# The opening of a gated-attention and FFN kernel: state sums of units 0 to 3 as prefix sums in PSUM, and another split and order of the first weight conversions

## The chip, the cores and the metric

The kernel runs on one core of a Trainium2 chip. The metric is the device time of one execution in microseconds (us). A core has a matrix engine (TensorE, PE in the rows, its weight loads PEld), a vector engine (VectorE, DVE), an activation engine (ScalarE, ACT), GpSimd (POOL) and SyncE (SP), which issues most transfers. TensorE writes to PSUM, eight banks of 2 KB for each of 128 partitions; the other engines read it from there.

## The reference

A recurrence over 768 positions for 4 batches of 8 heads of 48 dimensions, and then a feed-forward layer with a Gelu on the 3072 rows of 384 that come out:

```python
for t in range(S):
    state = alpha[:, :, t, :, None] * state + einsum('bhd,bhe->bhde', k[:, :, t], v[:, :, t])
    y[:, :, t] = einsum('bhd,bhde->bhe', q[:, :, t], state)
x = y.transpose(0, 2, 1, 3).reshape(B * S, H * D)
h = x @ w_in                                  # 384 -> 2048
out = (0.5 * h * (1 + erf(h / sqrt(2)))) @ w_out
```

## The kernel before

**Units.** The 3072 rows are 12 groups g of 256 positions, three to a batch; a group is two units (u = 0, 1) of four heads, so there are 24 units n. For a unit, VectorE makes running products of alpha forward (two scans of 256, L320) and backward (L333), multiplies q by the forward one (L326) and k by the backward one (L339). TensorE makes the scores in four chunks of 64 positions and turns k round (L360, L368). VectorE masks the scores (L427), ACT copies the turned k (L421). `inside` then multiplies the scores by v (L450) and, in the same bank, makes for each chunk j the sum of k times v over the chunk, 48 columns for each of 16 small matmuls (L469). These run on four quarters of the array, two halves of the rows by two halves of the columns. `chain` on VectorE adds the four sums up one after the other into the states before chunk 1, 2, 3 and after chunk 3 (L487 for the first of a batch, L489). `outer` multiplies q by these states (L519) and adds them to the bank. `carry` (L494) takes the last state to the next group.

**x.** What `inside` and `outer` leave in a unit's bank is x. It is used as two roundings, a high half (ACT copy, L599) and a low half, the rest: by VectorE as a difference (L603), or "by product": TensorE subtracts the high half from the bank with a matrix of -1 (L612) and ACT copies what is left (L616). `X_BY_PRODUCT` lists the units that do the second. A small transfer spreads spare rows of x (L625) before a step of the group can start.

**Weights.** w_in and w_out come as 16 pieces a to p of 768 KB, in turns (a is w_in's first, b w_out's first). Each is converted by ACT (top bits, L274), VectorE (join, L278), ACT (high half, L288), and its low half by VectorE (L291) or, for the pieces in `BY_PRODUCT` (numbers 1, 2, 3: b, c, d), by TensorE, four records of an identity matmul and two of a subtraction (`differ`, L300 and L301), and two ACT copies (L305). The two top buffers are used in turns, so the conversion of a piece starts behind the join of the piece two before it.

**Steps.** A step (g, f) multiplies a group's x by the pair of pieces f (L635, 18 matmuls of 256 columns), takes a Gelu, and multiplies by w_out's pieces (L844). Step (0, f) needs pieces 2f and 2f+1, f = 1 thus c and d. The high half of x of unit 2 waits for the low halves of pieces a to e, since its place is theirs before.

**Order.** A planner in the kernel fixes each engine's order ahead of time. Each operation has a cost (`COST`), what it depends on, and a rank; at each moment of the plan an engine takes the ready operation with the lowest rank (a negative rank is urgent work, for which VectorE and ACT may be kept idle for a moment). Ranks come from the place in the string `ORDER`: digits are units, letters pieces. SP's loads and fetches use the same ranks. Engines then work through their lists in that order, with waits where data come late. While no step has begun, TensorE is kept busy with matmuls of no use (`turn_over`, L140).

Of the kernel before, what the change touches and what calls it, by code (L numbers as in the profile page):

```python
# [8 lines left out]
F32 = mybir.dt.float32  # L9
# [7 lines left out]
ALU = mybir.AluOpType  # L17
# [2 lines left out]
STAGE = 3  # L20
SHIFT = 3
WARM = (1, 1, 4, 4, 2, 2)
BY_PRODUCT = (1, 2, 3)
EARLY = 2
JOINED = 5
FLIPPED = 6
SEAM = 0.22
HOLD = 0.35
U_RANK, HI_RANK = 0.5, 0.4
X_BY_PRODUCT = (1, 2)  # L30
STEPS_BY_PRODUCT = 2
LOOK, EARLY_LOOK = 1.5, 1.0
RATE = 360.0
XB = 3
# [1 line left out]
SLOW = 1.0  # L36
COST = dict(
    turn=0.3, head=0.75, body=0.95, tail=0.49, sel=0.6, sel2=1.0, ends=0.22, differ=1.2, half=0.34, minus=0.4, gminus=0.35, rest=0.5, rest2=1.0,
    scan=0.65, scan2=0.65, back0=0.86, back=0.71, times=0.62, q=1.35, scores=1.24, scores1=0.69, flip=0.72, over=0.56, move=0.35, moves=1.4, kn=0.52, mask=0.62, mask1=0.4, kn1=0.36, inside=1.28, chain=1.1, outer=0.77, carry=0.22,
    xh=0.6, xl=0.72, spread=2.0, check=0.85, load=2.6, fetch=0.4, u=1.0, c0=0.56, c1=0.89, c2=0.56, c3=0.95, c4=0.92,  # L40
    hi=0.82, lo=0.89, gemm1=2.12, gelu=0.51, low=0.62, most=1.4, last=0.69, part=1.0,
    wide1=2.1, wide2=2.07, wpart=1.1, quick1=2.45, quick2=1.42, comb1=0.36, comb3=1.08, chi=0.98, clo=1.2, wsum=0.72, wcomb=0.52, whi=0.52, wlo=0.65, gather=1.5, wend0=1.39, wend1=1.16, wend2=3.69,
)
ORDER = "0 1 a b c 2 d 3 e f 4 g h i j k 5 l m n o p"


@with_exitstack
def gla_then_gelu_ffn(ctx: ExitStack, tc: tile.TileContext, q, k, v, alpha, qg, kg, ag, vg, w_in, w_out, out):
    nc = tc.nc
    B, H, D, S = q.shape  # L50
    NF, P, NK, _ = w_in.shape
    DM, DFF = NK * P, NF * P
    NT = B * S
    C = 128
    G = 2 * C
    CS = C // 2
    NCH = G // CS
    DP = 64
    NPAIR = H // 2
    NU = NPAIR // 2  # L60
# [4 lines left out]
    GPB = S // G  # L65
# [6 lines left out]
    const = ctx.enter_context(tc.tile_pool(name="const", bufs=1))  # L72
# [40 lines left out]
    ybank = ps_y.tile([P, 2, BANK], F32, name="ybank")  # L113
# [40 lines left out]
    ends = const.tile([P, NG * NU, 2], F32, name="ends")  # L154
# [11 lines left out]

    states = []
    for u in range(NU):
        states.append([const.tile([P, 2, D], F32, name=f"state{u}_{i}") for i in range(NCH + 1)])

    mask = const.tile([P, CS], F32, name="mask")
    nc.gpsimd.memset(mask, 1.0)
    for half in range(2):
        r = slice(half * CS, (half + 1) * CS)
        nc.gpsimd.affine_select(
            out=mask[r],
# [166 lines left out]
    def ends_batch(g, j):  # L343
        return g % GPB == GPB - 1 and j == NCH - 1
# [89 lines left out]
    def inside(g, u):  # L434
        d = cur[g, u]
        ybank = y_of(NU * g + u)
        vn = vbuf[g % NB]
        spare = () if g else (0, 1)[: u + 1]
        for i in spare:
            nc.tensor.matmul(  # L440
                ybank[:, i, :G], lhsT=zeros, rhs=products[:, :G], start=True, stop=False, skip_group_check=True
            )
        for j in range(NCH):
            for i in range(2):
                r = slice(i * CS, (i + 1) * CS)
                for h in range(2):
                    rows = D if i in spare else DP
                    o = slice((h ^ i) * DP, (h ^ i) * DP + rows)
                    e = (2 * u + h) * D
                    nc.tensor.matmul(  # L450
                        ybank[o, i, j * CS : (j + 1) * CS],
                        lhsT=vn[r, j, e : e + rows],
                        rhs=d["ss"][r, h, j, :],
                        start=(j == 0 and i not in spare),
                        stop=(j == 0 and g % GPB == 0),
                        skip_group_check=True,
                    )
        if NU * g + u < FLIPPED:
            kn = d["kn"].rearrange("p b (c h d) -> p b c h d", c=2, h=2)
        for j in range(NCH):  # L460
            if ends_batch(g, j):
                continue
            t = 2 * C + j * D
            for i in range(2):
                r = slice(i * CS, (i + 1) * CS)
                for h in range(2):
                    o = slice(h * DP, (h + 1) * DP)
                    e = (2 * u + h) * D
                    nc.tensor.matmul(  # L469
                        ybank[o, i, t : t + D],  # L470
                        lhsT=d["kn"][r, h, j].rearrange("p b d -> p (b d)") if NU * g + u >= FLIPPED else kn[r, j // 2, j % 2, h],
                        rhs=vn[r, j, e : e + D],
                        start=False,
                        stop=True,
                        skip_group_check=True,
                    )

    def chain(g, u):
        d = cur[g, u]
        ybank = y_of(NU * g + u)  # L480
        st = states[u]
        for j in range(NCH):
            if ends_batch(g, j):
                continue
            new = ybank[:, :, 2 * C + j * D : 2 * C + (j + 1) * D]
            if g % GPB == 0 and j == 0:
                d["chain"] = nc.vector.tensor_copy(st[1], new)  # L487
            else:
                d["chain"] = nc.vector.tensor_tensor(out=st[j + 1], in0=new, in1=st[j], op=ALU.add)  # L489

    def carry(g, u):
        if ends_batch(g, NCH - 1):
            return
        nc.vector.scalar_tensor_tensor(  # L494
            out=states[u][0],
            in0=states[u][NCH],
            scalar=1.0 / MID,
            in1=cur[g, u]["pe"].unsqueeze(2).to_broadcast([P, 2, D]),
            op0=ALU.mult,
            op1=ALU.mult,  # L500
        )
# [7 lines left out]
    def outside_part(g, u):  # L509
        d = cur[g, u]  # L510
        ybank = y_of(NU * g + u)
        for j in range(NCH):
            if g % GPB == 0 and j == 0:
                continue
            t = slice(j * CS, (j + 1) * CS)
            for i in range(2):
                for h in range(2):
                    r, o = (slice(a * DP, a * DP + D) for a in (h, h ^ i))
                    ins = nc.tensor.matmul(  # L519
                        ybank[o, i, t],  # L520
                        lhsT=states[u][j][r, i],
                        rhs=d["qt"][r, i, t],
                        start=False,
                        stop=True,
                        skip_group_check=True,
                    )
                    tc.add_manual_dep(
                        ins.ins,
                        d["chain"].ins.name,
                        mybir.DependencyInfo(mybir.DependencyClass.Sync, mybir.DependencyReason.DATA),  # L530
                        reason="row tiles of one bank",
                    )
# [167 lines left out]
    sums = {}  # L700
# [303 lines left out]
    def op(*args, **kw):  # L1004
        ops.append(Op(*args, **kw))
        return ops[-1]

    load, ready_x, unit, wops, x_last = {}, {}, {}, {}, {}
    gemms = {}

    def plan_unit(n):
        g, u = divmod(n, NU)
        d = unit[n] = {}
        p, pp_ = unit.get(n - 1, {}), unit.get(n - 2, {})
        r = unit_rank[n]
        fns = {}
# [5 lines left out]
        old = unit.get(n - NB * NU, {})  # L1022
# [5 lines left out]
        if u == NU - 1:  # L1028
            d["load"].cost += 0.4
            d["load"].kb += 393  # L1030
        half = op("DVE", "scan", start, [d["load"], p.get("q"), p.get("keys"), p.get("ends")], rank=r)
        d["scan"] = op("DVE", "scan2", lambda: fns["f"](1), [half], rank=r)
        d["ends"] = op("ACT", "ends", lambda: fns["e"](), [d["scan"]], rank=-0.5)
        d["q"] = op("DVE", "times", lambda: fns["q"](), [d["scan"]], rank=r)
        before = unit.get(n - 3, {})
        half = op("DVE", "back0", lambda: fns["b"](0), [d["scan"], *([before["xh"], before["xl"]] if "out" in before else [])], rank=r)
        d["back"] = op("DVE", "back", lambda: fns["b"](1), [half], rank=r)
# [2 lines left out]
        of_y = [yp.get("out", yp.get(x)) for x in ("xh", "xl")]  # L1040
        if n >= FLIPPED:
            flip = op("DVE", "flip", lambda: flipped(g, u), [d["keys"], p.get("away")], rank=r)
            d["away"] = op("SP", "move", lambda: flip_out(g, u), [flip], rank=r - 50, lands=2.6, kb=262)
            back = op("SP", "moves", lambda: flip_back(g, u), [d["away"], p["kn"]], rank=r - 50, lands=4.5, kb=524)
# [31 lines left out]
        else:  # L1076
            d["mask"] = op("DVE", "mask", lambda: masked(g, u), [d["scores"], rp.get("inside")], rank=-1)
            d["kn"] = op("ACT", "kn", lambda: turned_out(g, u), [d["scores"], rp.get("inside"), d["mask"]], rank=-1)
        d["inside"] = op("PE", "inside", lambda: inside(g, u), [d["mask"], *of_y], rank=r)
        if n >= NU:  # L1080
            d["inside"].deps.append(d["kn"])
        else:
            d["inside"].soon = [d["kn"]]
        if n >= SPLIT:
            d["scores"].bank = (d["mask"],)
        d["chain"] = op("DVE", "chain", lambda: chain(g, u), [d["inside"], pp_.get("carry")], rank=-1 if n else 1.5)
        if n == 1:
            op("PE", "sel2", lambda: [selected(sbank[:, i, :G], i) for i in range(2)], [d["inside"], unit[0]["zh"]], rank=-1)
        d["outer"] = op("PE", "outer", lambda: outside_part(g, u), [d["chain"], ops[-1] if n == 1 else None], rank=r)
# [9 lines left out]
        elif g > NSB and (g - NSB) % 2:  # L1099
            k = (g - NSB) // 2  # L1100
# [67 lines left out]
    low_of, state = {}, {"g": None, "run": 0, "evac": None, "more": 0}  # L1168
# [320 lines left out]
    t = 0.0  # L1489
    idle = 0  # L1490
    while True:
        moved = False
        for e in ("DVE", "ACT", "PE", "SP", "POOL"):
            if free_at[e] <= t + 1e-9:
                o = choose(e, t)
# [13 lines left out]
        t = min(later_on)  # L1509
# [8 lines left out]
    for o in plan:  # L1518
# [5 lines left out]
        out=outside[:, n_units:],  # L1524
        in0=ends.rearrange("p n i -> p (n i)"),
# [89 lines left out]
```

## Time and profile before

| | |
|---|---|
| median of 3 runs | 486.96 us (486.9 to 487.24) |
| profiled execution | 488.16 us, its span 486.6 us |
| TensorE busy | 475.8 us, 98% of the span |
| VectorE, ACT busy | 332.3 us (68%), 223.5 us (46%) |
| granted TensorE clock, mean | 0.998 |

The span runs from the first to the last instruction. A busy TensorE is one with a matmul in flight, so it may still be filled better. The kernel has one long stretch in which TensorE is busy without a break, and an opening of some 50 us in which transfers, conversions and the first units share the engines; the change lies in the opening.

### The profile page before, as it was taken

The numbers are of one execution on the slowest core, as the hardware profiler recorded it, in microseconds if no ns is written. First come the engines' busy times: TensorE is split into PE (matmuls) and PEld (weight loads), VectorE is DVE, ScalarE is ACT, GpSimd is POOL, SyncE is SP. The second block draws the span as 40 slices with busy tenths as digits, with TensorE's granted clock in tenths as the row PEclk, the third lists the DMA queues.
The fourth block names the chain that finished last, engine by engine and source line by source line (L and its number), as shares of the span: only waits on it lengthen the run. The fifth ranks groups of instructions, "written<-read, shape, count | busy, mean of one in ns | idle before, by whom it ended". The sixth has DMA issues, their size and how long they took to land.

```text
span 486.6 us, 12615 instructions
## 1 busy us (share of the span) xinstructions
PE 475.8 (98%) x5315; PEld 414.5 (85%) x5315; DVE 332.3 (68%) x655; ACT 223.5 (46%) x426; POOL 7.4 (2%) x21
## 2 busy tenths in 40 slices
PE   8999999999999999999999999999999999999995
PEld 5778999999999999977778877888888888888883
DVE  6988999988878897888952265795555444544441
ACT  4788865354534444444442345353344343334331
POOL 2000000000000000000000000000000000000000
PEclk9999999999999999999999999999999999999999
DMA  8996674555546454564430030000010000100002
GB/s 291 394 359 220 204 245 123 164 177 179 168 145 199 151 178 123 164 208 150 128 96 1 1 126 10 9 1 1 1 66 0 1 0 1 65 1 1 1 1 72
DMA packets 33809, 53.80 MB, mean 111 GB/s; under 512 B 4272, under 2 KB 15344, under 8 KB 33744
## 3 DMA queue, kind: packets, MB, share of 16 engines
q1 hardware_dynamic: 32096, 47.86, 30.2%
q0 software_dynamic: 880, 3.93, 2.2%
q10 hardware_dynamic: 768, 1.11, 0.7%
q8 instruction: 44, 0.72, 0.6%
q14 instruction: 21, 0.17, 0.1%
HBM read 41.29 MB, written 9.44 MB: 104 GB/s over the span
## 4 chain that ended last, share of the span: by engine, by line
PE 85%; DMA 6%; ACT 4%; DVE 2%; issue 1%; ACTq 0%; SPq 0%
PE hw L652 28%; PE accw L667 12%; PE acc L844 11%; PE hp L635 10%; PE accw L760 10%; PE sbank L760 6%; DMA st<-in_moe_w_out_dram 5%; PE sbank L519 2%; PE sbank L450 2%; DMA qd<-in_qg_dram 1%; PE sbank L469 1%; ACT top L274 1%; PE sh L360 1%; DVE wil L291 1%; ACT ghi L819 1%
## 5 line engine op out<-in xcount | busy, mean ns | idle before, releaser
L652 PE MATMUL hw<-x,wih 128*128 128x512 f32 x288 | 91.1, 397 | 0.0
L819 ACT ACTIVATE ghi<-hw 128x512 fp32r<-128x512 f32 x64 | 38.1, 595 | 105.7 <-PE hw L652 105.6
L834 DVE TENSOR_TENSOR glo<-h,ghi 128x512 fp32r<-128x512 f32 x38 | 26.2, 689 | 51.8 <-ACT h L824 51.8
L652 PEld LDWEIGHTS hw<-x,wih 128*128 128x128 f32 x288 | 52.0, 188 | 10.7
L652 PE MATMUL hw<-x,wil 128*128 128x512 f32 x144 | 56.9, 395 | 0.0
L844 PE MATMUL acc<-woh,ghi 128*128 128x384 f32 x128 | 44.2, 346 | 0.9 <-ACT ghi L819 0.8
L844 PE MATMUL acc<-wol,ghi 128*128 128x384 f32 x128 | 43.1, 337 | 0.0
L834 DVE TENSOR_TENSOR glo<-hw,ghi 128x512 fp32r<-128x512 f32 x26 | 17.9, 687 | 32.6 <-ACT hw L824 32.4
L819 ACT ACTIVATE ghi<-hp 128x512 fp32r<-128x512 f32 x32 | 19.1, 596 | 43.7 <-PE hp L635 43.7
L753 ACT CAST qd<-ad 128x1024 fp32r<-128x1024 f32 x19 | 20.0, 1051 | 34.0 <-DVE ad L750 34.0
L635 PE MATMUL hp<-x,wih 128*128 128x256 f32 x192 | 35.3, 283 | 0.0
L333 DVE TENSOR_TENSOR_SCAN rp<-ad,rp,bottom 128x255 f32<-128x255 f32 x48 | 33.9, 738 | 0.9
L635 PE MATMUL hp<-two_x,wih 128*128 128x256 f32 x192 | 34.4, 280 | 0.0
L756 DVE TENSOR_TENSOR ad<-ad,qd 128x1024 fp32r<-128x1024 f32 x19 | 23.3, 1225 | 15.5 <-ACT qd L753 15.5
L320 DVE TENSOR_TENSOR_SCAN pp<-ad,bottom 128x256 f32<-128x256 f32 x48 | 30.8, 666 | 4.5 <-DMA ad<-in_ag_dram 4.5
L652 PEld LDWEIGHTS hw<-x,wil 128*128 128x128 f32 x144 | 27.0, 187 | 6.6
L667 PE MATMUL accw<-ghi,woh 128*128 128x512 f32 x78 | 31.4, 402 | 0.0
L667 PE MATMUL accw<-ghi,wol 128*128 128x512 f32 x78 | 30.6, 393 | 0.0
L635 PEld LDWEIGHTS hp<-x,wih 128*128 128x128 f32 x192 | 30.0, 189 | 0.4 <-issue 0.2
L652 PE MATMUL hw<-two_x,wih 128*128 128x512 f32 x96 | 30.0, 394 | 0.0
L635 PEld LDWEIGHTS hp<-two_x,wih 128*128 128x128 f32 x192 | 29.8, 188 | 0.0
L844 PE MATMUL acc<-woh,glo 128*128 128x384 f32 x128 | 28.7, 345 | 0.0
(251 smaller groups left out, 1087.6 us busy)
## 6 DMA issues: line engine op xcount, KB each, us to landing
st<-in_moe_w_in_dram SPq DMA_DIRECT2D x8, 768.0 KB, 7.4
st<-in_moe_w_out_dram SPq DMA_DIRECT2D x8, 768.0 KB, 7.6
qd<-in_qg_dram SPq DMA_DIRECT2D x23, 256.0 KB, 3.9
ad<-in_ag_dram SPq DMA_DIRECT2D x23, 256.0 KB, 3.2
kd<-in_kg_dram SPq DMA_DIRECT2D x23, 256.0 KB, 4.3
vn<-in_vg_dram SPq DMA_DIRECT2D x12, 416.0 KB, 6.0
fd<-fl SPq DMA_DIRECT2D x18, 256.0 KB, 2.1
kx<-fd SPq DMA_DIRECT2D x72, 64.0 KB, 3.7
```

The lines of the kernel that those rows point to most:

```text
L320: nc.vector.tensor_tensor_scan(pp[:, i], at[:, i], bottom, MID, ALU.mult, ALU.max)
L333: nc.vector.tensor_tensor_scan(rp[:, i, G - 2 :: -1], at[:, i, G - 1 : 0 : -1], bottom[:, 1:], rp[:, i, G - 1 :], ALU.mult, ALU.max)
L450: nc.tensor.matmul(ybank[o, i, j * CS : (j + 1) * CS], lhsT=vn[r, j, e : e + rows], rhs=d["ss"][r, h, j, :], start=(j == 0 and i not in sp ...
L635: nc.tensor.matmul(hp[:, j, :], lhsT=a[:, j, i * P : (i + 1) * P], rhs=x[:, i, :], start=(start and m == 0), stop=(stop and (j, i, n) in t ...
L652: nc.tensor.matmul(h, lhsT=a[:, j, i * P : (i + 1) * P], rhs=x[:, i, part], start=(i == 0 and n == 0), stop=(i == NK - 1 and n == 2),)
L667: nc.tensor.matmul(acc[i], lhsT=w[:, j, e], rhs=a, start=(f == 0 and k == 0 and w is wo_hi[f2]), skip_group_check=mixed, stop=(f == NF - 1 ...
L753: nc.scalar.copy(quick["hi"], quick["t"])
L756: nc.vector.tensor_tensor(out=quick["lo"], in0=quick["t"], in1=quick["hi"].bitcast(F32), op=ALU.subtract)
L760: nc.tensor.matmul(to, lhsT=a[x], rhs=b[y], start=(start and n == 0), stop=True, skip_group_check=True)
L819: nc.scalar.activation(ghi, hp, AF.Gelu)
L834: nc.vector.tensor_tensor(out=glo, in0=hp, in1=ghi.bitcast(F32), op=ALU.subtract)
L844: nc.tensor.matmul(acc[t], lhsT=a[:, j, t * C : (t + 1) * C], rhs=w[:, j, :], start=(first and j == 0 and k == 0 and w is wo_hi[f]), stop= ...
```

## The change

`inside` gives the moving operand v of chunk j a repeated view: it writes the product not to one place of 48 columns but to the places of chunk j and of all chunks after it (w = 4, 3, 2, 1 of them), in units 0 to 3. So the bank holds the sums over chunks 0 to j, and `chain` is one copy (first group) or one addition with the old state repeated (second group). The states of a unit become one tile. Pieces c and d and unit 2's x leave the lists of work by product. In `ORDER`, piece c moves from before unit 2 to behind unit 3. Unit 2's forward scans and its product with q get rank 1.5, between unit 1 and piece a. Two costs are new.

```diff
-BY_PRODUCT = (1, 2, 3)
+BY_PRODUCT = (1,)
+SUMMED = 4
-X_BY_PRODUCT = (1, 2)
+X_BY_PRODUCT = (1,)
+FORWARD = {2: 1.5}
...
+    inside1=1.63, chain1=0.52
-ORDER = "0 1 a b c 2 d 3 e f 4 g h i j k 5 l m n o p"
+ORDER = "0 1 a b 2 d 3 c e f 4 g h i j k 5 l m n o p"
...
-        states.append([const.tile([P, 2, D], F32, name=f"state{u}_{i}") for i in range(NCH + 1)])
+        states.append(const.tile([P, NCH + 1, 2, D], F32, name=f"states{u}"))
...
+        sums = NCH - ends_batch(g, NCH - 1)
+        for j in range(sums):
             t = 2 * C + j * D
+            w = sums - j if NU * g + u < SUMMED else 1
...
-                        ybank[o, i, t : t + D],
+                        ybank[o, i, t : t + w * D].rearrange("p (n d) -> p n d", n=w),
...
-                        rhs=vn[r, j, e : e + D],
+                        rhs=vn[r, j, e : e + D].unsqueeze(1).to_broadcast([CS, w, D]),
...
+        if NU * g + u < SUMMED:
+            new = ybank[:, :, 2 * C : 2 * C + sums * D].rearrange("p i (j d) -> p j i d", d=D)
+            to = st[:, 1 : sums + 1]
+            if g % GPB == 0:
+                d["chain"] = nc.vector.tensor_copy(to, new)
+            else:
+                old = st[:, :1].to_broadcast([P, sums, 2, D])
+                d["chain"] = nc.vector.tensor_tensor(out=to, in0=new, in1=old, op=ALU.add)
+            return
...
+        rf = FORWARD.get(n, r)
-        half = op("DVE", "scan", start, [d["load"], p.get("q"), p.get("keys"), p.get("ends")], rank=r)
+        half = op("DVE", "scan", start, [d["load"], p.get("q"), p.get("keys"), p.get("ends")], rank=rf)
...
-        d["inside"] = op("PE", "inside", lambda: inside(g, u), [d["mask"], *of_y], rank=r)
+        d["inside"] = op("PE", "inside1" if n < SUMMED else "inside", lambda: inside(g, u), [d["mask"], *of_y], rank=r)
-        d["chain"] = op("DVE", "chain", lambda: chain(g, u), [d["inside"], pp_.get("carry")], rank=-1 if n else 1.5)
+        d["chain"] = op("DVE", "chain1" if n < SUMMED else "chain", lambda: chain(g, u), [d["inside"], pp_.get("carry")], rank=-1 if n else 1.5)
```

## Rows read from the trace of the kernel before

**Rows 1.** The page, busy time, share of the span and instructions of each engine.

```profile
PE 475.8 (98%) x5315; PEld 414.5 (85%) x5315; DVE 332.3 (68%) x655; ACT 223.5 (46%) x426; POOL 7.4 (2%) x21
```

**Rows 2.** By stretch, length: busy PE, weight loads, DVE, ACT, POOL; clock; DMA; GB/s.

```profile
...
10.00:20.00 10.00, 9.30 (x220) 7.29 (x222) 8.94 (x22) 6.51 (x11) 0.00 (x0) 1.00 1.04 398
20.00:30.00 10.00, 9.18 (x98) 6.95 (x98) 8.73 (x16) 7.88 (x17) 0.00 (x0) 1.00 1.04 393
30.00:40.00 10.00, 10.00 (x233) 8.50 (x232) 9.44 (x21) 9.08 (x18) 0.00 (x0) 1.00 0.77 277
40.00:50.00 10.00, 9.17 (x165) 8.10 (x165) 8.98 (x14) 8.72 (x18) 0.00 (x0) 1.00 0.68 211
50.00:60.00 10.00, 10.00 (x76) 10.00 (x75) 8.85 (x16) 8.06 (x14) 0.00 (x0) 1.00 0.63 231
...
```

**Rows 3.** Waits of TensorE, 0 to 50 us: for whom, total, times, longest.

```profile
...
PE acc L844 <- ACT ghi L819: 0.8, 1, 0.8
PE differ L300 <- ACT wil L305: 0.8, 1, 0.8
...
```

**Rows 4.** Timeline: the matmuls of piece c's low half (start, length, idle before).

```profile
...
23.52 0.84 PE L300 MATMUL differ<-st,ident 128*128 128x384 f32 x2
...
25.35 0.95 PE L300 MATMUL differ<-st,ident 128*128 128x384 f32 x2 [0.82 <-ACT wil L305]
...
```

**Rows 5.** The chain that ended last: start, length, what.

```profile
...
26.30 0.17 PE differ L301
...
29.79 0.68 PE differ L300 x2
30.47 0.18 PE differ L301
30.65 0.76 PE differ L300 x2
31.41 0.18 PE differ L301
31.59 0.62 PE ybank L450 x32
32.22 0.45 PE ybank L469 x32
...
35.04 2.35 PE hp L635 x18
...
```

**Rows 6.** Timeline of TensorE around the subtraction of unit 2's x.

```profile
...
38.39 0.38 PE L612 MATMUL ybank<-z,minus 128*128 128x256 f32 x1
...
38.72 0.39 PE L191 MATMUL hp<-ghi,minus 128*128 128x512 f32 x1
...
```

**Rows 7.** Groups by shape, 0 to 55 us: count, busy us, mean ns, idle before.

```profile
...
L278 DVE SCALAR_TENSOR_TENSOR st<-st,top 128x768 int32<-128x768 int32 x9 | 8.5, 947 | 0.0
...
L320 DVE TENSOR_TENSOR_SCAN pp<-ad,bottom 128x256 f32<-128x256 f32 x12 | 7.9, 678 | 4.5 <-DMA ad<-in_ag_dram 4.5
...
L333 DVE TENSOR_TENSOR_SCAN rp<-ad,rp,bottom 128x255 f32<-128x255 f32 x11 | 7.7, 736 | 0.2
...
L288 ACT CAST wih<-st 128x768 fp32r<-128x768 f32 x5 | 4.5, 906 | 1.2 <-DVE st L278 1.2
...
L291 DVE TENSOR_TENSOR wil<-st,wih 128x768 fp32r<-128x768 f32 x4 | 3.8, 946 | 0.0
...
L489 DVE TENSOR_TENSOR state<-ybank,state 128x96 f32<-128x96 f32 x10 | 2.6, 255 | 0.5 <-PE ybank L469 0.2
...
L427 DVE TENSOR_TENSOR ss<-ybank,mask 128x512 f32<-128x512 f32 x2 | 1.4, 690 | 1.6 <-PE ybank L368 1.6
...
```

**Rows 8.** Timeline: two waits for transfers, and unit 1's adds.

```profile
...
17.17 0.69 DVE L320 TENSOR_TENSOR_SCAN pp<-ad,bottom 128x256 f32<-128x256 f32 x1 [0.79 <-DMA ad<-in_ag_dram]
...
18.99 0.84 DVE L489 TENSOR_TENSOR state<-sbank,state 128x96 f32<-128x96 f32 x3
...
20.57 1.08 ACT L274 CAST top<-st 128x768 f16<-128x768 bf16 x1 [1.40 <-DMA st<-in_moe_w_out_dram]
...
```

More of the change, by code (lines that the diff above doesn't have):

```diff
@@ L38 @@
     turn=0.3, head=0.75, body=0.95, tail=0.49, sel=0.6, sel2=1.0, ends=0.22, differ=1.2, half=0.34, minus=0.4, gminus=0.35, rest=0.5, rest2=1.0,
-    scan=0.65, scan2=0.65, back0=0.86, back=0.71, times=0.62, q=1.35, scores=1.24, scores1=0.69, flip=0.72, over=0.56, move=0.35, moves=1.4, kn=0.52, mask=0.62, mask1=0.4, kn1=0.36, inside=1.28, chain=1.1, outer=0.77, carry=0.22,
+    scan=0.65, scan2=0.65, back0=0.86, back=0.71, times=0.62, q=1.35, scores=1.24, scores1=0.69, flip=0.72, over=0.56, move=0.35, moves=1.4, kn=0.52, mask=0.62, mask1=0.4, kn1=0.36, inside=1.28, inside1=1.63, chain=1.1, chain1=0.52, outer=0.77, carry=0.22,
     xh=0.6, xl=0.72, spread=2.0, check=0.85, load=2.6, fetch=0.4, u=1.0, c0=0.56, c1=0.89, c2=0.56, c3=0.95, c4=0.92,
@@ L459, in inside @@
             kn = d["kn"].rearrange("p b (c h d) -> p b c h d", c=2, h=2)
-        for j in range(NCH):
-            if ends_batch(g, j):
-                continue
+        sums = NCH - ends_batch(g, NCH - 1)
+        for j in range(sums):
             t = 2 * C + j * D
+            w = sums - j if NU * g + u < SUMMED else 1
             for i in range(2):
@@ L481, in chain @@
         st = states[u]
-        for j in range(NCH):
-            if ends_batch(g, j):
-                continue
+        sums = NCH - ends_batch(g, NCH - 1)
+        if NU * g + u < SUMMED:
[7 more added lines that the diff above has]
+            return
+        for j in range(sums):
             new = ybank[:, :, 2 * C + j * D : 2 * C + (j + 1) * D]
             if g % GPB == 0 and j == 0:
-                d["chain"] = nc.vector.tensor_copy(st[1], new)
+                d["chain"] = nc.vector.tensor_copy(st[:, 1], new)
             else:
-                d["chain"] = nc.vector.tensor_tensor(out=st[j + 1], in0=new, in1=st[j], op=ALU.add)
+                d["chain"] = nc.vector.tensor_tensor(out=st[:, j + 1], in0=new, in1=st[:, j], op=ALU.add)
     def carry(g, u):
@@ L494, in carry @@
         nc.vector.scalar_tensor_tensor(
-            out=states[u][0],
-            in0=states[u][NCH],
+            out=states[u][:, 0],
+            in0=states[u][:, NCH],
             scalar=1.0 / MID,
@@ L520, in outside_part @@
                         ybank[o, i, t],
-                        lhsT=states[u][j][r, i],
+                        lhsT=states[u][r, j, i],
                         rhs=d["qt"][r, i, t],
@@ L1030, in plan_unit @@
             d["load"].kb += 393
-        half = op("DVE", "scan", start, [d["load"], p.get("q"), p.get("keys"), p.get("ends")], rank=r)
-        d["scan"] = op("DVE", "scan2", lambda: fns["f"](1), [half], rank=r)
+        rf = FORWARD.get(n, r)
+        half = op("DVE", "scan", start, [d["load"], p.get("q"), p.get("keys"), p.get("ends")], rank=rf)
+        d["scan"] = op("DVE", "scan2", lambda: fns["f"](1), [half], rank=rf)
         d["ends"] = op("ACT", "ends", lambda: fns["e"](), [d["scan"]], rank=-0.5)
-        d["q"] = op("DVE", "times", lambda: fns["q"](), [d["scan"]], rank=r)
+        d["q"] = op("DVE", "times", lambda: fns["q"](), [d["scan"]], rank=rf)
         before = unit.get(n - 3, {})
```

## The prediction

> **What bounds the kernel now.** I read the engines' shares first: TensorE is busy for 98% of the span, no other engine for more than 68% [rows 1]. The table by stretch says where the missing 2% lie: from 50 us on TensorE is busy in all of nearly every stretch, and what it lacks is in the opening, 0.70 us in 10 to 20, 0.82 us in 20 to 30, 0.83 us in 40 to 50 [rows 2]. The granted clock is 1.00 in each of these rows. So a saving has two ways to reach the end: less work for TensorE at any place behind about 20 us, or less waiting in the opening. The waits of TensorE name the two gaps: 0.8 us before a `differ` matmul, for the copy that empties its bank, and 0.8 us before the second product of the step (0,2), for a Gelu [rows 3]. VectorE is the second engine to watch: 8.7 to 9.4 us of each 10 in the opening [rows 2], and the transfers fill their engines until 30 us at some 395 GB/s (398 and 393 [rows 2]).
>
> **Part 1, low halves of pieces c and d (`BY_PRODUCT`).** Each cost TensorE four `differ` records and two subtractions. For piece d they stand in the chain as 0.68 + 0.18 + 0.76 + 0.18 = 1.80 us [rows 5]. Piece c went worse: its first half starts at 23.52, its second only at 25.35, after the 0.82 us wait [rows 4], and ends at 26.47 [rows 5]: 2.95 us. Out of TensorE's row go 1.80 + 2.95 = 4.75 us, 0.82 of them waiting. Against that VectorE gets two subtractions of 0.95 us [rows 7], ACT loses four copies.
>
> **Part 2, x of unit 2 (`X_BY_PRODUCT`).** Two matmuls go, from 38.39 to the next work at 38.72: 0.33 us [rows 6]. VectorE gets one subtraction over 128x512, at the price of its mask of that shape, 0.69 us [rows 7].
>
> **Part 3, prefix sums.** The 16 small matmuls of L469 stay 16, with 192, 144, 96 and 48 columns in place of 48 each: 480 column positions in place of 192. Before shows no such wide one. They can't get cheaper, since each streams as much or more. The lower end goes by columns: a `differ` half is 384 columns in two records, 0.68 us [rows 5], so 1.77 ns a column; the four quarters of the array work side by side, 480 x 1.77 = 0.85 us against the 0.45 us of L469 [rows 5], +0.40 a unit. By the same count the 64-column group (256 positions) would be 0.45 us and took 0.62 in the chain [rows 5], so a group can carry up to 0.17 more than its columns. The upper end is plain proportion, 0.45 x 2.5 = 1.13, +0.68. I take +0.45, since the wide matmuls are nearer to the 384-column row than to the small ones: four units, +1.8 us (1.6 to 2.7).
>
> What it buys is on VectorE: four additions of 0.255 us (1.13 us for a unit in the chain of units 2 and 3) become one over 384 columns. From 96 columns at 0.255 and 512 at 0.69 [rows 7] a column is 1.05 ns, so 0.255 + 288 x 1.05 = 0.55 us; 0.5 less for each unit by the sum of four (1.02 us), 2 us in all. On the path from `inside` to `outer` +0.45 and -0.5 cancel. VectorE as a whole: +1.9 +0.7 -2.0, +0.6 us.
>
> **Part 4, the order.** Piece c's fetch goes behind unit 2, piece d and unit 3 on SP's queue. Unit 2's data then have one piece (768 KB, 0.79 MB, at 395 GB/s 2.0 us) less ahead of them. Its first scan waited for them until 17.17, 0.79 us idle [rows 8]; they would be there at about 15.2, and rank 1.5 puts both scans and the product with q ahead of the conversions. The cover is thin: where unit 1's sum comes due in the middle it has rank -1 and goes first; before, a scan and a low half stood ahead of it, and its adds ran from 18.99 [rows 8]. I expect unit 1's `outer` and with it the opening up to step (0,0) about 1.5 us earlier. Behind c on the queue are e's fetch (no later by bytes), and h's, which waits for c's low half.
>
> When is piece c ready, which (0,1) needs? Count VectorE from 15.2: four forward scans 2.7, four backward 2.9, four products 2.75 (taken at the mask's 0.69, the same shape), two masks 1.4, low halves of a and d 1.9, joins of b, d and c 2.85, two sums 1.1 each at its duration in [rows 7]: 15.6 us, so 30.8. Reciprocals, carries and waits for TensorE or ACT come to some 1.5 us by the difference between busy and 10 us in [rows 2]; then c's high half on ACT, 0.91, and its low half, 0.95, with hand-overs: about 34.2. Unit 3's `inside` needs no piece and fits before it. So (0,1) would start near 34.2 and take its 2.35 us [rows 5]: done at 36.5. Before, (0,1) and unit 3's `inside` were both done at 38.39 [rows 6]. That is 1.9 us, and the 0.33 us of part 2 follow: 2.2 us.
>
> The same by work: -4.75 -0.33 +1.8 = -3.3 us of TensorE's row, and against it new waiting for c and for unit 3's keys, which the date of 34.2 puts at about 1.2 us: -2.1. I take -2.0. Behind 38 us I book nothing: the 0.8 us gap of (0,2) may close, since unit 3 is done earlier and step (1,0) can stand in, or a new one may open, because e's conversion follows c's (they share a buffer) and x of unit 2 waits for e.
>
> The profiled execution took 488.16 us, its span 486.6 with 1.56 around it; the sum makes it 486.2. The median of the runs is 486.96, so 485.0.
>
> **The rivals.** (A) The forecast, with 484.0 to 486.0: chance 0.50.
>
> (B) The gain is refilled. The removed matmuls lie at 23 to 31 us, where weight loads fill only 6.95 us of 10 against 10.00 in 50 to 60 [rows 2]: TensorE's row is long there partly because it has nothing else ready. If VectorE, with 0.6 us more to do, sets the date of (0,1) at 35.5 to 36, only 0 to 0.9 us are left: 486.0 to 487.9. For it: VectorE at 9.44 of 10 in 30 to 40. Against it: 0.79 us of its waiting for unit 2's data goes. Chance 0.24. The Trainium skill ("Trainium Kernel Development and Optimization", Performance Expectations) says that matmul busy time is a bad metric and the busy share of weight loads a good one; by that rule this stretch is not bound by TensorE and the time would come out as in B. The trace half agrees: 6.95 against 9.18 in the same stretch.
>
> (C) Slower: TensorE runs dry for want of piece c. Units 2 and 3 and (0,0) are all it has until then, and c's join, high and low half hang behind the VectorE work of the two units and behind ACT. It decides at 36.4: (0,1) started there ends with 0.33 us to make up at 38.7, the old date. A low half of c at 38.0 gives +1.6, 488.6. For it: one engine order by hand, so any late transfer holds all behind it, as piece d's did, 1.40 us on ACT [rows 8]. Against it: 2.2 us of slack to 36.4. Chance 0.13.
>
> (D) More: (0,1) early, the prefix at its low end and the gap of (0,2) closed: -2.0 -0.2 -0.8, 483 to 484. Chance 0.13. That the wide matmuls don't run side by side at all would be another +2.5 us a unit (480 x 1.77 x 4 = 3.4 us); the 0.62 us of 16 matmuls at 64 columns, 1.8 us if one behind the other, speak against it, and it has no more than a part of C.
>
> **How the numbers follow.** The likeliest is A, 485.0. To leave out 2 in 10 I cut half of D and most of C: 483.6 to 487.8; the prefix's upper end (+0.9) is inside. About 0.2%, 0.97 us, is what a measurement of this kernel can tell from no change. Faster: A and D, 0.63. Same: B, 0.24. Slower: C, 0.13.
>
> **What would show it.** Right: no `differ` records for c and d; L469 at 0.85 to 0.95 us a unit; one VectorE operation of 0.55 us for each sum; unit 2's scans at 15 to 16; (0,1) at 33.5 to 35; TensorE's busy time 1.5 to 2.5 us less and its gaps not larger. Wrong: a gap of TensorE at 27 to 34 waiting for unit 2's or 3's keys or for c's low half; new gaps at 38 to 48 from e's conversion; L469 above 1.2 us.

## The result: slower, by a wait that stands behind the opening

| | before | after |
|---|---|---|
| median | 486.97 us (486.11 to 488.98, 14 runs) | 490.62 us (488.78 to 493.63, 14 runs) |
| ratio to before | | 1.008, 95% interval 1.0065 to 1.0096 |
| profiled execution, its span | 488.16, 486.6 us | 492.06, 490.5 us |
| TensorE busy | 475.8 us | 476.7 us |
| mean granted clock | 0.998 | 0.990 |

The change costs 3.65 us by the medians, where 2.0 us of gain were forecast. The executions of after spread, and time and mean clock go together: 488.78 us at 0.998, 493.63 us at 0.987. The fastest of them is still slower than the median of before by 1.8 us. The profiled one lies 1.4 us above their median.

The opening itself went as forecast. Timeline of after (start, length, engine, line, operation, what it writes and reads; in brackets the idle time of its engine before it and what ended it):

```profile
15.43 1.27 DVE L322 TENSOR_TENSOR_SCAN pp<-ad,bottom 128x256 f32<-128x256 f32 x2
...
17.77 0.56 DVE L489 COPY states<-sbank 128x384 f32<-128x384 f32 x1 [0.35 <-PE sbank L471]
...
27.76 1.02 PE L471 MATMUL ybank<-vn,kn 64*64 64x192 f32 x32
28.68 0.69 PE L362 MATMUL sbank<-qd,kd 48*64 48x64 f32 x32
...
32.62 0.69 PE L452 MATMUL sbank<-ss,vn 64*64 64x64 f32 x32 [0.68 <-ACT kn L423]
...
34.08 0.51 PE L645 MATMUL hp<-x,wih 128*128 128x256 f32 x2
...
36.43 0.67 PE L529 MATMUL sbank<-qd,states 48*48 48x64 f32 x32
```

Unit 2's scans start at 15.43 in place of 17.17 [rows 8]. A sum is one VectorE operation of 0.56 us. The prefix matmuls of a unit hold TensorE for 0.92 us (27.76 to 28.68), against 0.45 [rows 5]. The product of step (0,1) runs from 34.08, and behind it unit 3's `outer` from 36.43. One new gap came, 0.68 us before 32.62, where TensorE waits for unit 3's turned keys; it lies inside the 1.2 us of new waiting that the forecast allowed. Up to 38 us TensorE is busy for 34.23 us, in before for 34.26.

The loss lies behind that. By stretch (length; busy PE, PEld, DVE, ACT, POOL; granted clock; DMA share; GB/s), to be read against [rows 2]:

```profile
20.00:30.00 10.00, 9.96 (x180) 8.44 (x171) 9.35 (x18) 8.28 (x15) 0.00 (x0) 1.00 1.04 393
30.00:40.00 10.00, 9.19 (x172) 8.31 (x173) 9.95 (x18) 9.42 (x18) 0.00 (x0) 1.00 0.94 338
40.00:50.00 10.00, 7.87 (x70) 7.07 (x69) 6.31 (x10) 6.49 (x12) 0.00 (x0) 0.86 0.37 132
45.00:50.00 5.00, 4.59 (x51) 4.20 (x52) 4.96 (x8) 4.43 (x9) 0.00 (x0) 0.72 0.00 0
48.00:50.00 2.00, 2.00 (x11) 2.00 (x11) 2.00 (x5) 2.00 (x4) 0.00 (x0) 0.50 0.00 0
50.00:55.00 5.00, 5.00 (x51) 4.75 (x53) 3.85 (x6) 3.73 (x8) 0.00 (x0) 0.94 0.55 189
100.00:110.00 10.00, 8.11 (x130) 7.97 (x134) 5.28 (x9) 4.28 (x10) 0.00 (x0) 0.83 0.15 49
```

In 20 to 30 the gap is gone; most of the 0.81 us that TensorE lacks in 30 to 40 is the wait for unit 3's keys. In 40 to 50 and in 100 to 110 TensorE lacks 2.13 and 1.89 us, all engines fall off together, and the clock falls to 0.86 and 0.83. The waits of TensorE over the whole span (for whom, from whom: total us, times, longest) name one reader for both:

```profile
PE acc L854 <- DVE glo L844: 4.0, 2, 2.2
```

The same stretch, engine by engine, with SP's and ACT's transfer issues (SPq, ACTq):

```profile
36.58 0.46 SPq L216 DMA_DIRECT2D ad<-in_ag_dram  x1
37.16 0.36 SPq L216 DMA_DIRECT2D qd<-in_qg_dram  x1
37.57 0.53 SPq L216 DMA_DIRECT2D kd<-in_kg_dram  x1
38.15 0.42 SPq L218 DMA_DIRECT2D vn<-in_vg_dram  x1
39.17 2.55 SPq L635 DMA_DIRECT2D two_x<-z  x3
...
39.56 0.61 ACTq L635 DMA_DIRECT2D two_x<-z  x1
40.21 0.59 ACT L197 CAST glo<-hp 128x512 fp32r<-128x512 f32 x1
42.40 1.16 ACTq L635 DMA_DIRECT2D two_x<-z  x2
43.61 0.58 ACT L834 ACTIVATE hp<-hp 128x512 f32<-128x512 f32 x1 [2.81 <-DMA qd<-in_qg_dram]
44.22 0.69 DVE L844 TENSOR_TENSOR glo<-hp,ghi 128x512 fp32r<-128x512 f32 x1 [3.66 <-ACT hp L834]
44.97 0.97 PE L854 MATMUL acc<-woh,glo 128*128 128x384 f32 x4 [1.72 <-DVE glo L844]
```

Read from the bottom: TensorE waits for VectorE's low half of the Gelu, VectorE for ACT's whole Gelu, and ACT computed nothing for 2.81 us, from 40.80 to 43.61; the last thing to land in that time was the load of unit 7's q. The Gelu doesn't read q. What stands ahead of it on ACT are two of the six copies, of 32 KB each, that spread group 1's spare rows (`spread`, L635): half of the six are issued by ACT (`eng = nc.scalar if h and g < NSB else nc.sync`).

The trace's records name, for each issue by SP or ACT, the counter that the transfer raises when it has arrived. There are eight of them, used in rotation, and an issue first waits for the transfer that had its counter before, eight issues back. The two copies have the counters of the loads of unit 7's alpha and q, which SP issued at 36.58 and 37.16. These landed at 42.33 and 42.98, and ACT issued the copies at 42.40 and 43.01. So of the 2.81 us some 1.7 were the hold, and 1.1 the two issues themselves, which took ACT 0.52 and 0.56 us.

At 100 us the same happens with group 2's copies and the load issued by SP from 92.12 (unit 9's). The counters of its k and v came free at 98.52 and 99.95, and the copies went out at 98.60 and 99.97, some 2.7 us of hold and 1.0 of issuing:

```profile
93.11 0.42 SPq L216 DMA_DIRECT2D kd<-in_kg_dram  x1
93.58 0.42 SPq L218 DMA_DIRECT2D vn<-in_vg_dram  x1
...
98.60 1.89 ACTq L635 DMA_DIRECT2D two_x<-z  x2
100.53 0.58 ACT L834 ACTIVATE hp<-hp 128x512 f32<-128x512 f32 x1 [3.80 <-DMA two_x<-z]
```

In before ACT issued its half of the copies too. Group 1's:

```profile
43.55 1.16 ACTq L625 DMA_DIRECT2D two_x<-z  x2
44.75 0.89 ACT L288 CAST wih<-st 128x768 fp32r<-128x768 f32 x1 [1.21 <-DVE st L278]
```

There ACT issued them as soon as it was done with the range check before them (43.35 + 0.19 us), so no load held them. Unit 3's low half of x ended at 43.52 there, at 39.70 in after, 3.8 us earlier. The issues were not free even so: with all copies on SP (below) this cast starts right behind the check, at 42.88, and the 0.83 us wait of TensorE for the Gelu of (0,2) [rows 3] is gone. Group 2's copies were held by a load in before already:

```profile
92.73 3.65 ACTq L625 DMA_DIRECT2D two_x<-z  x2
96.43 0.72 ACT L222 ACTIVATE junk<-ad,hi_b 128x512 uint8<-128x512 f32 x1 [6.07 <-DVE kd L339]
```

The second of the two has the counter of a load that SP issued at 89.52. It landed at 95.84, and the copy went out at 95.86, 2.6 us after the issue of the first had ended. What stood behind it was a range check, and TensorE has no wait from 88 to 106. So here a hold of ACT cost nothing by itself; in after half of a Gelu stood behind it, and TensorE came to need that half.

The rest of the loss is the clock. Of the two levels, 1.2 and 2.4 GHz, TensorE had the upper one until it had stood still for 1.72 us at 43.2 and 0.41 us at 45.9. In 45 to 50 the granted clock is 0.72, and in 48 to 50 it is 0.50, the lower level, though TensorE is busy all the time. Groups by shape in 40 to 50 (busy us, mean ns), first after, then the kernel of the last group of experiments, in which nothing stands still there:

```profile
L645 PE MATMUL hp<-two_x,wih 128*128 128x256 f32 x8 | 2.7, 433 | 0.0
L645 PE MATMUL hp<-two_x,wil 128*128 128x256 f32 x3 | 1.2, 415 | 0.0
```

```profile
L645 PE MATMUL hp<-two_x,wih 128*128 128x256 f32 x24 | 4.4, 282 | 0.0
L645 PE MATMUL hp<-two_x,wil 128*128 128x256 f32 x12 | 3.4, 280 | 0.0
```

The same matmul takes 433 and 282 ns. What is missing of the clock, times length, gives what was lost in this execution: 0.28 x 5 us in 45 to 50 and 0.06 x 5 in 50 to 55 behind the first stop, 0.17 x 10 in 100 to 110 behind the second, 3.4 us in all.

### The profile page after: what moved, and what is told of

The parts are those of the page before. It is cut to its first block, busy times and chain, and to the rows that moved or that the text cites. A ratio compares the mean times of both kernels' runs of the same rounds, so it can differ in the third digit from the quotient of the medians.

```text
span 490.5 us, 12555 instructions
## 1 busy us (share of the span) xinstructions
PE 476.7 (97%) x5297; PEld 415.6 (85%) x5297; DVE 333.9 (68%) x649; ACT 223.1 (45%) x420; POOL 7.4 (2%) x21
## 4 chain that ended last, share of the span: by engine, by line
PE 88%; DMA 5%; DVE 4%; issue 1%; ACT 1%; SPq 0%; ACTq 0%; DVEq 0%
PE hw L662 28%; PE acc L854 12%; PE hp L645 12%; PE accw L677 11%; PE accw L770 9%; PE sbank L770 5%; PE sbank L452 2%; DMA st<-in_moe_w_out_dram 2%; PE sbank L529 2%; PE sbank L471 2%; DMA two_x<-z 2%; DMA kd<-in_kg_dram 1%; PE sh L362 1%; PE ybank L362 1%; DVE glo L844 1%
## 5 line engine op out<-in xcount | busy, mean ns | idle before, releaser
L645 PE MATMUL hp<-two_x,wih 128*128 128x256 f32 x192 | 35.8, 287 | 0.0
L844 DVE TENSOR_TENSOR glo<-hp,ghi 128x512 fp32r<-128x512 f32 x30 | 20.7, 689 | 17.3 <-ACT hp L834 17.0
L645 PEld LDWEIGHTS hp<-two_x,wih 128*128 128x128 f32 x192 | 31.0, 195 | 0.0
```

Of the source, the lines that this page charges most:

```text
L645: nc.tensor.matmul(hp[:, j, :], lhsT=a[:, j, i * P : (i + 1) * P], rhs=x[:, i, :], start=(start and m == 0), stop=(stop and (j, i, n) in t ...
L844: nc.vector.tensor_tensor(out=glo, in0=hp, in1=ghi.bitcast(F32), op=ALU.subtract)
```

## The experiments

The theory to be tested: the time went into the hold of ACT (and what follows from it), and not into the parts of the change. The rivals: the copies are slow because of the traffic at that time, whoever issues them; or the parts themselves cost more than forecast.

**Copies issued by SP alone, in after and in before.**

```diff
-                eng = nc.scalar if h and g < NSB else nc.sync
+                eng = nc.sync
```

> The changed kernel, with ACT's share of the transfers that spread x (L635, groups 1 and 2) issued by SP. The order of every other instruction is the same. Theory (hold): in the changed kernel ACT idles 2.81 us before the whole Gelu at 43.61 and 3.80 us before the one at 100.53, because these two issues stand ahead of them in its order and wait for loads that were issued at 36.6 to 37.2 and at 93.1. TensorE idles 1.72 + 0.41 and 2.24 us behind that, and its granted clock is 0.72, 0.94 and 0.83 in the three rows that follow, 5 x 0.28 + 5 x 0.06 + 10 x 0.17 = 3.4 us. Without the hold 5 to 8 us of the changed kernel's 490.6 go: 483 to 486. Rival (weights late): TensorE would idle at 40 to 46 anyway, since piece c and with it e to h were moved back and VectorE has more to do; the time stays at 489 to 491. Rival (the wait only moves): SP now holds its loads behind the same wait; a stall appears some us later, 488 to 490.

> The kernel before, with ACT's share of the spreading transfers issued by SP: the control. Hold: in the kernel before ACT also waits at these issues (they end at 44.7 and at 96.4), but next to nothing urgent stands behind them; only the 0.8 us wait of TensorE for the Gelu of step (0,2) at 46.19 may be part of it. 486 to 487. If the issuing queue were worth something by itself, whatever the change, this one would gain as much as the other, 4 us or more.

After: 485.83 us (484.94 to 487.86), ratio to before 0.9986 (0.9971 to 1.0). Before: 486.87 us, 0.9995 (0.9983 to 1.0008). So 4.8 us of after hang on who issues half of the small copies of two groups, with every engine's order of compute as it was; in before nothing measurable does. The rival that weights come late is out. The stop of 2.81 us on ACT is gone (the Gelu's second half starts at 40.54), but some of the hold only moved:

```profile
39.28 4.66 SPq L635 DMA_DIRECT2D two_x<-z  x6
...
46.23 0.47 PE L645 MATMUL hp<-two_x,wih 128*128 128x256 f32 x2 [1.04 <-DMA two_x<-z]
```

SP now spends 4.66 us on the six copies behind unit 7's load, and step (1,0) waits 1.04 us for them. In three of its ten executions the mean clock was 0.994 or 0.995, and those took 486.89 to 487.86 us.

**ACT's share issued by GpSimd.**

```diff
-                eng = nc.scalar if h and g < NSB else nc.sync
+                eng = nc.gpsimd if h and g < NSB else nc.sync
```

> The changed kernel, with ACT's share of the spreading transfers issued by GpSimd, which has nothing else queued there, and whose transfers have completion counters of their own. Hold: like the SP variant, 483 to 486, and the transfers themselves start as soon as x is there, near 39.5 and 40, not at 42.4. If it is the data of x that came late, not the counter, the issue waits on GpSimd too.

486.66 us (485.18 to 488.69), ratio 0.9988 (0.9972 to 1.0005). ACT is free again and most of the loss is gone, with as many issuers of the copies as in after; the median lies 0.7 us above the range that was expected.

```profile
39.84 1.61 POOL L635 DMA_DIRECT2D two_x<-z  x3 [36.29 <-DVE rp L333]
40.32 0.61 ACT L834 ACTIVATE hp<-hp 128x512 f32<-128x512 f32 x1
```

The three copies go out from 39.84, as soon as x is there, though SP has issued unit 7's alpha, q and k ahead of them; in the trace GpSimd's transfers have counters of their own. So the data of x were not late, and the traffic didn't hold their issue. Step (1,0) waits for x for 2.0 us in place of 1.04. It is ACT's being held that costs, and not the number of queues.

**After without the prefix sums, ACT's copies kept.**

```diff
-SUMMED = 4
+SUMMED = 0
```

> The changed kernel without its prefix sums (SUMMED = 0: 48 columns for each small matmul, four additions for a unit), the rest of the change as it is, ACT issuing its share. The planner orders anew. By the prediction's prices TensorE has 4 x 0.45 to 0.55 us less to do and VectorE 2 us more in the opening. Hold: the spread of group 1 still falls behind the loads of units 6 and 7 by about the same distance, so a stall of 1 to 3 us in ACT near 42 us stays, 488 to 491. If the prefix sums were what costs the time, 486 or less.

488.17 us (486.86 to 490.0), ratio 1.0021 (1.0004 to 1.0039): 2.4 us better than after. Taken alone this speaks against the sums. But without them the order around the copies changes too (TensorE's longest wait in that trace is 2.4 us for ACT's copy of the Gelu's rest, and the clock in 40 to 45 is 0.76). The same comparison without the collision, further down, gives the opposite sign. A part can't be priced while it also decides who collides.

**The loads of units 7 and 9 behind the copies.** This takes away what the copies wait for and leaves their issuers alone (the planner makes its order anew around it):

```diff
+        if n in (7, 9):
+            d["load"].deps.append(ready_x[n // 4][1])
```

> After, with one edit: the loads of units 7 and 9 are issued behind the copies of x of groups 1 and 2 in place of ahead of them; ACT keeps its share of the copies. Hold theory (a copy waits for the transfer eight before it in program order): group 1's copies now stand eight behind transfers that landed before 37 us, so ACT isn't held at 40.2 to 42.4, the Gelu runs at about 40.8, TensorE's wait at 43 to 45 goes and with it the clock of 0.72 in 45 to 50. Of group 2's copies ACT's two then stand eight behind the small key copies of unit 7, issued at 94 to 97 and 3.7 us in landing, so some of the second wait (up to 2.2 us) and of its clock of 0.83 stays. Time 487 to 488. Rival (the copies wait because the transfers themselves are many at that time): the same bytes are asked for within the same few us, both waits stay, 490.6.

485.33 us (485.12 to 486.06), ratio 0.9965 (0.9951 to 0.9978): 5.3 us better than after, with the same issuers and the same bytes. This run alone doesn't rule out the traffic, since it also takes the load's bytes away from the copies' time; the counters above and GpSimd's copies do. ACT and its copies in this run, first stretch and second:

```profile
40.33 1.59 ACTq L635 DMA_DIRECT2D two_x<-z  x2
41.97 0.58 ACT L834 ACTIVATE hp<-hp 128x512 f32<-128x512 f32 x1 [1.13 <-issue]
...
93.71 1.44 ACTq L635 DMA_DIRECT2D two_x<-z  x2
95.20 0.58 ACT L834 ACTIVATE hp<-hp 128x512 f32<-128x512 f32 x1 [1.44 <-DMA kx<-fd]
```

The 1.13 and 1.44 us in which ACT computed nothing are nearly all issuing. The 2 us that I expected to stay at the second place did not: the key copies there went out from 91.08, and the two whose counters ACT's copies have landed at 93.64 and 94.62, so the second copy was held for 0.4 us.

**One load at a time.** The same edit with `n == 7`, then with `n == 9`:

> After, with unit 7's load alone behind group 1's copies (unit 9's stays ahead of group 2's; ACT keeps its share). Hold theory: the first wait, at 43 to 45 us, and the clock drop behind it go, the second, at 100 us, stays with its own drop. In the trace of after the first is 1.72 + 0.41 us of waiting and some 1.7 us at a lower clock (0.28 of 5 us, 0.06 of 5 us), the second 2.24 us and 1.7 us (0.17 of 10 us); that execution was 1.4 us above the median, so each is worth some 2.6 us of the 5.3 between 490.62 and 485.33: 488.0. If the two hang together, so that a step saved at the first only lengthens the second: 490.

> The other half: unit 9's load alone behind group 2's copies. Hold theory: the first wait and drop stay, the second go: 488.0. If the second is only what the first left late: little change, 490.

488.01 us (486.55 to 489.76) and 487.74 us (486.55 to 489.69), against 490.62 with neither and 485.33 with both. The ratios are 1.0015 (1.0003 to 1.0028) and 1.0012 (1.0 to 1.0025). The gains are 2.61 and 2.88 us, 5.49 together, and both edits at once give 5.29 (by the ratios 6.5 and 5.6 us, the same within the intervals): two separate losses that add up. Each trace keeps just its own hold, in the first of these runs at 94.79, in the second at 42.92, and behind it one stop of TensorE, of 1.86 and 2.02 us:

```profile
94.79 1.74 ACTq L635 DMA_DIRECT2D two_x<-z  x2
96.58 0.58 ACT L834 ACTIVATE hp<-hp 128x512 f32<-128x512 f32 x1 [3.41 <-DMA two_x<-z]
```

```profile
42.92 1.16 ACTq L635 DMA_DIRECT2D two_x<-z  x2
44.12 0.58 ACT L834 ACTIVATE hp<-hp 128x512 f32<-128x512 f32 x1 [3.10 <-DMA qd<-in_qg_dram]
```

The clock behind the stop differs, first run, then second:

```profile
95.00:105.00 10.00, 8.14 (x162) 7.62 (x160) 5.64 (x11) 4.78 (x12) 0.00 (x0) 1.00 0.18 56
```

```profile
45.00:50.00 5.00, 4.52 (x45) 3.96 (x46) 4.97 (x9) 4.43 (x8) 0.00 (x0) 0.54 0.01 3
50.00:55.00 5.00, 5.00 (x35) 5.00 (x35) 3.49 (x6) 2.77 (x7) 0.00 (x0) 0.78 0.46 139
```

The profiled execution of the first (486.55 us, the fastest of its twelve) has its stop and no lower clock at all; that of the second (489.69 us, the slowest) lost 3.4 us of clock behind one stop. So a drop "of its own" behind each stop, which was expected, is not what every execution shows.

**Both edits, in after and in before.** Loads behind the copies, and all copies by SP:

> The same edit together with all copies issued by SP. Hold theory: in the run with SP's copies alone, six of them were held behind the load of unit 7 from 39.28 to 43.94, and step (1,0) waited 1.04 us for x. Ahead of the load they go out in some 2.4 us, x is there at about 44, the wait goes: 1.0 us less than with SP alone, 484.8, and no drop of the clock in any execution. Rival (the wait comes from TensorE being early, and the 4.7 us are the copies' own price): as with SP alone, 485.8.

> Control: before, with the two edits of the 484.84 us run (loads of units 7 and 9 behind the copies of x, all copies issued by SP) and nothing of the change. If those edits only take away a collision that the change made, before gains nothing from them: 486.9, as with SP's copies alone. If they are a gain of their own, before falls too, to 485.5 or less, and that much of the 2.4 us is not the change's.

After: 484.84 us (483.97 to 485.26), ratio 0.9951 (0.9937 to 0.9965). It is the fastest kernel here, and faster than before beyond the interval. Before: 486.40 us, ratio 0.9984 (0.9974 to 0.9993), so 0.6 to 0.8 us of it belong to the two edits; that part of the expectation was wrong. The change itself, both sides free of the collision, is worth 0.9951 / 0.9984 = 0.9967, 1.6 us, some 0.8 to 2.4 us by the two intervals. After in this form has no gap and no lower clock where it had both:

```profile
40.00:50.00 10.00, 10.00 (x124) 9.55 (x127) 9.53 (x16) 8.42 (x15) 0.00 (x0) 1.00 0.57 162
...
100.00:110.00 10.00, 10.00 (x115) 9.93 (x108) 9.22 (x19) 4.97 (x13) 0.87 (x1) 1.00 0.49 172
```

**Which part earns the 1.6 us.** First single parts with SP's copies only, each against 486.87: the prefix sums alone, then the low halves of c, d and unit 2's x alone.

> Before, with the prefix sums of units 0 to 3 alone (part 3) and SP's copies; low halves, order and scans as before. To stand against before with SP's copies, 486.87. Work theory (TensorE's row sets the time): the wide matmuls cost about 0.5 us a unit, +1.5 to +2.0: 488.4 to 488.9. Path theory (in the opening VectorE's row sets the time, and there a sum takes 0.55 us in place of 1.1): 486.0 to 486.9.

> Before, with the low halves of pieces c and d and of unit 2's x moved to VectorE (parts 1 and 2), and SP's copies; sums, order and scans as before. To stand against before with SP's copies, 486.87. Work theory: TensorE loses 4.75 + 0.33 us, most of it comes out: 482.5 to 484.0. Path theory: VectorE gets 2.6 us more in an opening where it is at 8.7 to 9.4 of each 10 us, and TensorE waits for it instead: 486.9 to 488.5.

487.38 us (486.89 to 488.21), ratio 1.0007 (0.9998 to 1.0016), which lies between the two ranges expected, and 489.84 us (486.95 to 491.64), ratio 1.0042 (1.0023 to 1.0061). The second can't be read as a price: the conversions had met the collision again, at another place.

```profile
43.29 3.39 SPq L635 DMA_DIRECT2D two_x<-z  x4
```

```profile
50.01 0.77 PE L645 MATMUL hp<-two_x,wih 128*128 128x256 f32 x2 [3.55 <-DMA two_x<-z]
```

So the parts were taken again on top of both edits, against 486.40: parts 1 and 2 alone, part 3 alone, and all but part 3 (`SUMMED = 0`).

> Before, with parts 1 and 2 alone (low halves of c, d and unit 2's x on VectorE), the loads of units 7 and 9 behind the copies of x, all copies by SP; order, scans and sums as before. To stand against before with the last two edits, 486.4. If the conversions alone lost only by the collision: 489.84 less the 3.55 us of waiting and 1.5 us of clock, 484.8 or less. If VectorE's row holds them back (2.6 us more for it in an opening where it is at 8.7 to 9.4 of each 10 us): 486.4 to 487.5.

> Before, with the prefix sums alone (part 3), the loads of units 7 and 9 behind the copies of x, all copies by SP. To stand against before with the last two edits, 486.4. By work: four times 0.5 us more for TensorE, 487.9 to 488.4. If the sums help only where VectorE sets the dates, as with the conversions on it: no gain here, 486.4 to 487.4. If they are worth the same 1.9 us by themselves: 484.5.

> The kernel of the 484.84 us run, without the prefix sums (part 3): the sums of units 0 to 3 by 16 equal matmuls and four additions, as before. Parts 1, 2 and 4 stay. Work theory (the wide matmuls are a price of 0.5 us a unit on TensorE's row): 483 to 483.5. Path theory (in the opening VectorE sets the date of every step, and a sum costs it 0.5 us more, 2.0 us for the four units): 486 to 487. The prediction booked both and let them cancel on the path: 484.8.

| on top of both edits | us | ratio to before, 95% | TensorE busy, idle in 0 to 48 (profiled execution) |
|---|---|---|---|
| nothing of the change | 486.40 | 0.9984 (0.9974 to 0.9993) | 474.4, 4.58 us |
| parts 1 and 2 | 486.58 | 1.0004 (0.9986 to 1.0022) | 473.6, 6.35 us |
| part 3 | 486.61 | 0.9984 (0.9975 to 0.9993) | 476.3, 3.48 us |
| parts 1, 2 and 4 | 486.75 | 0.9997 (0.9985 to 1.0009) | 472.5, 6.31 us |
| all four | 484.84 | 0.9951 (0.9937 to 0.9965) | 473.5, 3.63 us |

No part that was run by itself gains anything; part 4 alone and parts 3 and 4 together were not run. (The executions with parts 1 and 2 alone run from 485.6 to 490.24 us, the longer ones at a mean clock of 0.989 to 0.994; the profiled one is of these, so its busy time holds some lower clock.) Parts 1, 2 and 4 save 1.9 us of TensorE's work (472.5 against 474.4) and return 1.7 us as waiting up to 48 us (6.31 against 4.58), 2.4 us up to 300 (7.26 against 4.85). The prefix sums alone cost 1.9 us of work and take 1.1 us of waiting away. Together the work falls by 0.9 us and the waiting too, by 0.95 us. With the conversions on VectorE the sums are worth 1.9 us (486.75 to 484.84). Where they act is seen in 30 to 40, first without them, then with:

```profile
30.00:40.00 10.00, 7.47 (x160) 6.29 (x159) 9.79 (x22) 9.51 (x16) 0.00 (x0) 1.00 0.73 250
```

```profile
30.00:40.00 10.00, 9.47 (x175) 8.32 (x175) 10.00 (x18) 9.40 (x18) 0.00 (x0) 1.00 0.93 314
```

VectorE is full in both (9.79 and 10.00 of 10), and TensorE has 2.0 us less idle time with the sums. That it gets there what the sums save VectorE is my reading of these rows; whether the sums need the conversions for it, or only the new order, is not shown, since parts 3 and 4 were not run without them.

## Why the prediction was wrong

**What held.** Parts 1 and 2 took the records out that the prediction listed. Part 3 came to 0.47 us a unit on TensorE (0.92 less 0.45) where 0.45 was taken, 0.40 to 0.68 given; on VectorE to 0.55 or 0.56 where 0.55 was taken. Part 4's dates were 15.2, 34.2 and 36.5, and 15.43, 34.08 and 36.43 came. Rival C, TensorE dry for want of piece c, needed a start of (0,1) behind 36.4, which didn't come. Of the signs of being wrong that the prediction lists, a gap for unit 3's keys came, 0.68 us, inside what was booked. So up to 38 us the forecast was right, and the loss is not rival C's.

**The step that failed** is "Behind 38 us I book nothing". It looked for what is late next among VectorE's conversions and unit 2's x, and missed that an earlier unit 3 brings its own transfers forward. In place of nothing, the runs showed two holds of ACT of 1.7 and 2.7 us, two stops of TensorE of 1.72 and 2.24 us, and 4.8 us that go when SP issues ACT's copies. Of a step that moves, each transfer must be followed to the engine that issues it and to what stands behind the issue there. The copies of x went from 43.55 us on ACT to a place between the Gelu's two halves, right behind the load of unit 7. All that was needed was in the program and the trace of before: the line that gives ACT half of the copies, the load, the Gelu between them, and even a hold of the kind, ACT's two issues of 3.65 us at 92.73. The planner that makes the order didn't see it either: to it `spread` is an operation of SP alone, with a cost and no wait.

**The size.** By the profiled executions after takes 490.5 us and the form without the collision 482.9, 7.6 us less. TensorE's idle time up to 300 us is 8.39 and 3.88 us (4.5 us), its busy time 476.7 and 473.5 us (3.2 us), which answers to the 3.4 us by the clock. So in that execution about two fifths of the loss were not waiting but a lower clock after the waiting. It is one of the slower ones: those at a mean clock of 0.998 took 488.78 to 490.18 us, so the waiting alone makes after slower than before, and how much clock is lost behind it changes from execution to execution. The prediction had seen a clock of 1.00 in all its rows and booked none of it.

**The sum behind the forecast.** -2.0 us was near what the change alone is worth, 1.6 us without the collision. That is partly luck, since its terms were less right. The low halves were to take 1.80 + 2.13 + 0.33 = 4.3 us of busy time from TensorE (the 0.82 us of waiting left out); with the new order it fell by 1.9 us, and why by so little is open. The prediction took the prefix sums as a price on TensorE (+1.8, and 1.9 came) that "cancels" on the path, and the low halves as the gain. In the runs either alone gives nothing, and together with the order they give 1.6 us. The likely reason is that the one pays for the other: VectorE, full in 30 to 40, has room for the low halves because the sums cost it 2 us less. No run shows this against an effect of the order with the sums. The account by work would have let each part stand alone at its own sum.

**Rival B**, a refilled gain, is what the conversions without the sums did: 1.9 us less of TensorE's work with parts 1, 2 and 4 bought no time. With all four parts it didn't come, and the loss of after is not of its kind.

**The issuing engine.** The Trainium skill ("DMA: Bandwidth & Descriptors", Issuing engines are not separate DMA queues) says that issuing from several engines saves only the time of issuing, which is usually small beside the transfer. The runs agree as far as it goes: before is 486.97 us with ACT's help and 486.87 us without. The Trainium skill (the same page, Anatomy of one DMA — SWDGE (gpsimd) path) says that the DMA engines don't wait for semaphores, and that any such wait is done by the issuing sequencer before it hands the transfer on. The trace agrees, for ACT as the issuer: its two copies went out 0.03 to 0.07 us after the loads ahead of them had landed (42.33 and 42.98), and ACT computed nothing until then.

## What to carry to other kernels

When a change makes a step earlier, list the transfers that it issues, the engine that issues each, the transfer that each has to wait for, and the compute that stands behind the issue; a transfer issued by a computing engine can hold a Gelu for a load that has nothing to do with it. Price the parts of a change only after such a collision is taken out: with it in place leaving out the sums looked like a gain of 2.4 us, without it like a loss of 1.9. And parts that each gain nothing can be worth 1.6 us together, here probably because one saves work on the second engine where the other adds it.

## What was not expected of the hardware

In the profile of after a stop of TensorE of some 2 us cost nearly as much again in clock (1.7 us for each by the rows): the granted clock was 0.72 in the 5 us behind the first, though TensorE was busy for 4.59 of them, and 0.83 in the 10 us around the second. It is not so each time: in the two runs with one load moved, a stop of 1.86 us cost no clock and one of 2.02 us cost 3.4 us. Each issue of a 32 KB copy took ACT 0.5 to 0.6 us in after, the hold left out. Of the small matmuls of L471, 48 columns took 0.21, 96 took 0.24, 144 took 0.29 and 192 took 0.33 us: four times the columns, 1.6 times the time.
